# Attention and MLP on one core: the first batch on one queue in order of need, the later loads on the Pool queue

## The chip, the cores and the metric

The kernel runs on one core of one Trainium2 chip. The metric is the device time of one execution in microseconds (us). Each kernel was run several times; a run is called slow when it is over 1.5% above the fastest run of the same kernel, and the other runs fast. A verdict is "the same" when the interval of the ratio lies within 2%, and "unclear" when it lies on both sides of that line.

The engines go by the profile's names: PE is the TensorE (matmul), PEld its weight loads, DVE the VectorE, ACT the ScalarE, POOL the GpSimd engine, SP the SyncE. SP and ACT issue transfers to hardware queues, POOL to a software queue; the profile prints these kinds beside each queue. The clock granted to PE is printed as a share of full speed (PEclk). "L433" is line 433 of the kernel in question, so line numbers differ between kernels.

## The reference, cut to what matters

```python
# q, k, v: (8 batches, 8 heads, 576 positions, 64), float32
scores = q @ k^T / 8;  mask = |i - j| <= 32
attn = softmax(where(mask, scores, -1e9))
x = (attn @ v) as (4608 tokens, 512)
h = x @ w_in                       # 512 -> 2048
g = s * relu(h)**2 + b
out = g @ w_out                    # 2048 -> 512, float32
```

## The kernel before

For each batch the kernel loads q, k and v to staging tiles (`STG`), casts them to bf16 (`NAT`, `VB`), and needs q and k transposed (`QT`, `KT`). Batches 0 and 1 (`b < NPE`) are loaded in chunks of 256 rows and transposed on the TensorE. Batches 2 to 7 are loaded in blocks of 128 rows and transposed by DMA. Attention runs in units of 192 queries and two head pairs; the MLP runs in token blocks, the first of 384, 128 and 256 tokens. The attention of later batches is spread between the MLP's matmuls.

A planner puts all tasks into one fixed order for each engine, by assumed costs and a key. At run time each engine keeps to this order: in the traces of two kernels planned alike (below) PE, DVE and ACT ran the same 2544, 483 and 331 instructions in the same order, though their loads landed at different times. So the instruction at the head of an engine waits, and everything behind it too.

```python
def load(b, n, blk, waits=()):          # v of all batches; q and k of batches 2 to 7
    ...
    return add(
        "pool" if n == "v" else "sp",
        lambda e: e.dma_start(
            STG[n][p0:p1, blk, :].rearrange("p (h d) -> p h d", h=H),
            src_of[n][b, :, s0:s0 + ns, :].rearrange("h s d -> s h d"),   # pieces of 64 float32
        ), ...)

def load2(b, n, c, waits=()):           # q and k of batches 0 and 1, pieces of 128 float32
    s0, ns = CHUNKS[c]
    return add("sp", lambda e: e.dma_start(
        STG[n][0:ns, 2 * c:2 * c + 2, :].rearrange("p a (h x) -> p (a h) x", h=NPAIR),
        src_of[n][b, :, s0:s0 + 2 * ns, :].rearrange("h (p r) d -> p h (r d)", r=2)), ...)

for n, c in (("q", 0), ("k", 0), ("k", 1), ("q", 1), ("k", 2), ("q", 2)):
    load2(0, n, c)
for blk in range(6):
    load(0, "v", blk)
...
wts = [load_weights("in" if i < 4 else "out", i % 4) for i in range(8)]   # on "pool"
...
def transpose_dma(b, n, blk):
    ...
    add("sp", lambda e: e.dma_start(dst[:, :, c0:c0 + ns], NAT[n][0:ns, blk, :], transpose=True),
        1250.0, reads=[("NAT", n, blk)], writes=grans(n, slot, s0, s0 + ns), ...)
...
# batch 1 may not load before the sixth weight has landed
load2(b, *x, waits=[wts[5]] if b == 1 else ())
```

The softmax here doesn't subtract the row's maximum and nothing guards it: scores larger than these inputs give would overflow.

Of the kernel before, what the change touches and what calls it, by code (L numbers as in the profile page):

```python
# [6 lines left out]
BF16 = mybir.dt.bfloat16  # L7
# [204 lines left out]
def bass_sliding_window_symmetric__then__act_starrelu_kernel(  # L212
# [23 lines left out]
    with ExitStack() as es:  # L236
# [51 lines left out]
        EVACS = [("act", "dve"), ("dve", "dve")]  # L288
# [6 lines left out]
        for b in range(B - 1, 0, -1):  # L295
            for t in range(NT3 - 1, -1, -1):
                for g2 in (1, 0):
                    nxt = min(nxt - PACE, 16 * first_block(b * S + 192 * t) - LEAD)
                    rel[b, t, g2] = nxt

# [12 lines left out]
        def load(b, n, blk, waits=()):  # L313

            if n == "v":
                p0, p1 = VROWS[blk]
                s0 = 192 * (blk // 2) - WIN + 128 * (blk % 2) + p0
            else:
                p0, p1 = 0, rows(blk)
                s0 = 128 * blk  # L320
            ns = p1 - p0
            return add(
                "pool" if n == "v" else "sp",
                lambda e: e.dma_start(  # L324
                    STG[n][p0:p1, blk, :].rearrange("p (h d) -> p h d", h=H),
                    src_of[n][b, :, s0:s0 + ns, :].rearrange("h s d -> s h d"),
                ),
                900.0 if n == "v" else 1070.0, writes=[("STG", n, blk)], waits=waits,
                key=-2000 if b == 0 and n == "v" and blk < 2 else key_of(b, -5),
                dma=("v" if n == "v" else "l", ns * 9.4))  # L330
# [4 lines left out]
        def load2(b, n, c, waits=()):  # L335
            s0, ns = CHUNKS[c]
# [3 lines left out]
                    STG[n][0:ns, 2 * c:2 * c + 2, :].rearrange("p a (h x) -> p (a h) x", h=NPAIR),  # L340
                    src_of[n][b, :, s0:s0 + 2 * ns, :].rearrange("h (p r) d -> p h (r d)", r=2),
                ),
                1000.0, writes=[("STG", n, 2 * c), ("STG", n, 2 * c + 1)], key=key_of(b, -5), waits=waits,
                dma=("l", 8 * ns * 26 / 16.0))
# [14 lines left out]
        for n, c in (("q", 0), ("k", 0), ("k", 1), ("q", 1), ("k", 2), ("q", 2)):  # L359
            load2(0, n, c)  # L360
        for blk in range(6):
            load(0, "v", blk)
# [37 lines left out]
        wts = [load_weights("in" if i < 4 else "out", i % 4) for i in range(8)]  # L400


        def cast_v(b, blk):
# [5 lines left out]
                380.0, reads=[("STG", "v", blk)] + pad, writes=[("VB", slot, blk)], key=key)  # L409
            if blk in (2, 4):  # L410
                add("dve", lambda e: e.tensor_copy(VB[slot][0:64, blk, :], STG["v"][64:128, blk - 1, :]),
                    380.0, reads=[("STG", "v", blk - 1)], writes=[("VB", slot, blk)], key=key,
                    accum=False)

        def grans(n, slot, lo, hi):
            return [(n + "T", slot, x) for x in range(max(0, lo) // 64, (min(S, hi) - 1) // 64 + 1)]
# [6 lines left out]
        def transpose_dma(b, n, blk):  # L423
# [4 lines left out]
                1250.0, reads=[("NAT", n, blk)], writes=grans(n, slot, s0, s0 + ns),  # L428
                dma=("t", 1000.0), key=key_of(b, max(0, 128 * blk - WIN) // 192 - 0.4))

        def cast2(b, n, c):
            ns = CHUNKS[c][1]
            add("dve", lambda e: e.tensor_copy(  # L433
                NAT[n][0:ns, 2 * c:2 * c + 2, :].rearrange("p r (h d) -> p r h d", h=H),
                STG[n][0:ns, 2 * c:2 * c + 2, :].rearrange("p a (g r d) -> p r (a g) d", r=2, d=D)),
                700.0, reads=[("STG", n, 2 * c), ("STG", n, 2 * c + 1)],
                writes=[("NAT", n, 2 * c), ("NAT", n, 2 * c + 1)], key=key_of(b, c - 0.5))
# [3 lines left out]
        def transpose_pe(b, n, c, banks, evacs):  # L441
            slot = b % 2
            s0, ns = CHUNKS[c]
            dst = QT[slot] if n == "q" else KT[slot]
            c0 = s0 + (0 if n == "q" else WIN)
            key = key_of(b, c - 0.4)
            for r in range(2):
                res, bank = banks[tcount["n"] % len(banks)]
                tcount["n"] += 1
                view = bank.bitcast(BF16)[:, 0:512].rearrange("p (g c) -> p g c", g=NPAIR)[:, :, 0:ns]  # L450
                to = dst[:, :, c0:c0 + 2 * ns].rearrange("p g (x r) -> p r g x", r=2)[:, r]
                add("pe", [lambda e, pr=pr, r=r, view=view: e.transpose(  # L452
                    view[:, pr, :], NAT[n][0:ns, 2 * c + r, pr * 128:(pr + 1) * 128], IDENT[0:ns, 0:ns])
                    for pr in range(NPAIR)],
                    270, reads=[("NAT", n, 2 * c), ("NAT", n, 2 * c + 1), "IDENT"], writes=[res], key=key)
# [3 lines left out]
                add(evac, fn, 200 + 4 * ns / 1.0, reads=[res],  # L459
                    writes=grans(n, slot, s0, s0 + 2 * ns), key=key, accum=(r == 1))  # L460
# [5 lines left out]
        def unit(b, t, g2, after):  # L466
# [7 lines left out]
            qk_res = grans("q", slot, q0, q0 + 192) + grans("k", slot, q0 - WIN, q0 + 192 + WIN)  # L474
            qk_res.append(("KTPAD", slot))
            fns = []
            for u, pr in enumerate(prs):
# [14 lines left out]
                700.0, reads=[("E", e_), "MASK"], writes=[("E", e_)], key=key)  # L492
# [30 lines left out]
        for b in range(B):  # L523
# [3 lines left out]
            if b < NPE:  # L527
                steps = [("q", 0), ("k", 0), 0, ("k", 1), ("q", 1), 1, ("k", 2), ("q", 2), 2]
                if b > 0:
                    for x in steps:  # L530
                        if isinstance(x, tuple):
                            load2(b, *x, waits=[wts[5]] if b == 1 else ())
# [13 lines left out]
            for x in steps:  # L546
                if isinstance(x, tuple):
                    cast2(b, *x)
                    transpose_pe(b, *x, banks, EVACS[b])
                    continue  # L550
                cast_v(b, 2 * x)
                cast_v(b, 2 * x + 1)
# [137 lines left out]
```

## Time and profile before

| | before |
|---|---|
| time, median of 3 runs (range) | 345.61 us (345.03 to 349.01) |
| PE busy | 314.9 us of a span of 344.8 us |
| DMA transposes, issue to landing, median (largest) | qt 3.6 (7.5), kt 3.5 (8.7) us |
| first mask multiply, first MLP matmul | 20.77, 29.96 us |

From the page of the profile: the DMA queues (packets, megabytes, time of the packets as a share of 16 engines), and the chain of waits that ended last.

```profile
q1 hardware_dynamic: 100416, 35.40, 50.1%
q0 software_dynamic: 7360, 13.64, 20.3%
...
PE 83%; DMA 7%; DVE 4%; issue 2%; SPq 1%; ACT 1%; DVEq 0%
```

Two queues carry nearly everything: the hardware queue in small packets (35.40 MB over 100416 packets is 353 B each) and the software queue in large ones (1853 B each). The chain is 83% PE: the kernel is bound by the TensorE. Where PE is not full shows in windows of ten us. The columns are the window, then for PE, PEld, DVE, ACT and POOL the busy us and the number of instructions, then the granted clock of PE, the DMA share and GB/s.

```profile
10.00:20.00 10.00, 3.31 (x33) 2.50 (x31) 4.88 (x8) 3.21 (x4) 6.24 (x9) 1.00 1.15 221
20.00:30.00 10.00, 8.21 (x121) 5.71 (x119) 9.68 (x20) 8.08 (x15) 2.32 (x4) 1.00 1.24 208
...
60.00:70.00 10.00, 9.85 (x102) 5.81 (x101) 8.30 (x21) 4.43 (x12) 0.78 (x1) 1.00 0.92 221
90.00:100.00 10.00, 6.33 (x67) 3.37 (x65) 7.50 (x19) 5.94 (x12) 2.07 (x3) 1.00 1.25 195
110.00:120.00 10.00, 9.84 (x92) 4.72 (x92) 5.96 (x14) 5.16 (x9) 1.17 (x2) 1.00 1.20 186
120.00:130.00 10.00, 9.79 (x84) 4.71 (x84) 8.68 (x19) 7.93 (x14) 1.58 (x2) 1.00 1.27 223
130.00:140.00 10.00, 9.95 (x84) 4.53 (x84) 8.02 (x20) 7.35 (x14) 2.37 (x3) 1.00 0.84 173
```

PE is idle in the first 30 us and again at 90 to 100 us; elsewhere it is close to 10. The reason at the start is on DVE. In its timeline (start, duration, instruction, and in brackets the idle time before it and what ended it) the first v cast waits 5.10 us, and a cast of q waits 4.28 us, with the first mask multiply (L490) behind it at 20.77.

```profile
8.18 0.67 DVE L408 CAST vb<-stgv 128x512 bf16<-128x512 f32 x1 [5.10 <-DMA stgv<-in_v_dram]
...
18.97 0.69 DVE L433 CAST natq<-stgq 128x1024 bf16<-128x1024 f32 x1 [4.28 <-DMA stgq<-in_q_dram]
...
20.77 0.69 DVE L490 TENSOR_TENSOR ex<-ex,mask 128x1024 bf16<-128x1024 bf16 x1
```

The hole at 90 to 100 us begins with this wait of PE (us in total, times, longest), for one transpose that landed late:

```profile
PE sc L480 <- DMA kt<-natk: 3.4, 1, 3.4
```

The last view is of DMA between 85 and 250 us: transfers by tile, issuing engine, count, size, and the median from issue to landing. In this stretch all q and k loads and all transposes are on SP.

```profile
out_dram<-outs SPq DMA_DIRECT2D x18, 256.0 KB, 2.9
stgq<-in_q_dram SPq DMA_DIRECT2D x17, 256.0 KB, 5.4
stgk<-in_k_dram SPq DMA_DIRECT2D x17, 256.0 KB, 5.7
...
qt<-natq SPq DMA_TRANSPOSE x28, 3.6
kt<-natk SPq DMA_TRANSPOSE x28, 3.5
```

Loads take about 5.5 us, transposes about 3.5.

### The profile page before, as it was taken

Reading aid. Unit: us, or ns where it says so; the run is one execution under the profiler, and the core shown is the slowest. Engines: PE = TensorE matmul, PEld = TensorE weight load, DVE = VectorE, ACT = ScalarE, POOL = GpSimd, SP = SyncE. Lnnn points to the kernel's source line nnn. Section 1 sums busy time; section 2 is a strip of 40 time slices with the busy share of each in tenths; the row PEclk is TensorE's granted clock in tenths of the full one; section 3 lists DMA queues with packets and bytes.
Section 4 is the critical chain, followed back from the end, with each engine's and each line's share of the span. In section 5 each row is a group of like instructions: output and inputs, shape, how many; then the busy total and the mean of one; then the engine's idle time right before and its main releaser. Section 6 shows DMA issues by size and latency. Waiting matters only on the chain.

```text
span 344.8 us, 6390 instructions
## 1 busy us (share of the span) xinstructions
PE 314.9 (91%) x2504; PEld 159.8 (46%) x2544; DVE 211.2 (61%) x475; ACT 181.6 (53%) x327; POOL 48.1 (14%) x68
## 2 busy tenths in 40 slices
PE   0459999999869999999999999999999999999995
PEld 0345556565435444444444444444444444445542
DVE  2676578888958688768677677653445345433321
ACT  1357634476747586755667665653466355533310
POOL 8812041001305011202022000000000000000000
PEclk9999999999999999999999999999999999999999
DMA  7999999979998998997999997630000010010111
GB/s 192 235 211 206 212 250 195 223 168 183 237 165 182 202 219 180 200 206 147 206 204 185 209 205 168 140 75 32 31 32 30 32 61 32 22 41 30 62 50 75
DMA packets 107807, 49.46 MB, mean 143 GB/s; under 512 B 87552, under 2 KB 100864, under 8 KB 107776
## 3 DMA queue, kind: packets, MB, share of 16 engines
q1 hardware_dynamic: 100416, 35.40, 50.1%
q0 software_dynamic: 7360, 13.64, 20.3%
q8 instruction: 20, 0.33, 0.4%
q14 instruction: 11, 0.09, 0.1%
HBM read 36.70 MB, written 9.44 MB: 134 GB/s over the span
## 4 chain that ended last, share of the span: by engine, by line
PE 83%; DMA 7%; DVE 4%; issue 2%; SPq 1%; ACT 1%; DVEq 0%
PE w L572 36%; PE o L590 35%; DMA stgq<-in_q_dram 4%; PE ss L503 4%; PE sc L480 4%; PE av L503 3%; DMA kt<-natk 3%; PE o L611 1%; DVE vb L408 1%; DVE xt L517 1%; SPq L339 1%; ACT ex L487 1%; PE sc L452 1%; DVE ex L490 1%; DVE natk L420 0%
## 5 line engine op out<-in xcount | busy, mean ns | idle before, releaser
L572 PE MATMUL w<-xt,win 128*128 128x512 bf16 (+3 forms) x689 | 146.3, 342 | 2.3 <-issue 1.1
L590 PE MATMUL o<-wout,gt 128*128 128x512 bf16 x551 | 140.4, 379 | 2.1 <-issue 1.1
L572 PEld LDWEIGHTS w<-xt,win 128*128 128x128 bf16 x704 | 62.8, 98 | 61.1 <-DVE xt L517 0.9
L590 PEld LDWEIGHTS o<-wout,gt 128*128 128x128 bf16 x576 | 53.4, 98 | 58.2 <-DVE outs L602 0.5
L324 POOL DMA_DIRECT2D stgv<-in_v_dram x48 | 38.9, 812 | 140.5 <-DVE vb L408 121.0
L487 ACT ACTIVATE ex<-sc 128x1024 bf16<-128x1024 f32 x48 | 49.1, 1022 | 10.5 <-PE sc L480 9.6
L490 DVE TENSOR_TENSOR ex<-ex,mask 128x1024 bf16<-128x1024 bf16 x48 | 33.1, 691 | 21.6 <-ACT ex L487 21.2
L578 ACT ACTIVATE r_26<-w 128x512 bf16<-128x512 f32 (+3 forms) x44 | 22.9, 520 | 28.2 <-PE w L572 26.2
L578 ACT ACTIVATE r_25<-w 128x512 bf16<-128x512 f32 (+3 forms) x44 | 22.8, 518 | 26.2 <-PE w L572 24.0
L578 ACT ACTIVATE r_27<-w 128x512 bf16<-128x512 f32 (+3 forms) x44 | 22.8, 519 | 23.3 <-PE w L572 22.0
L578 ACT ACTIVATE r_28<-w 128x512 bf16<-128x512 f32 (+3 forms) x44 | 22.8, 519 | 23.1 <-PE w L572 23.0
L510 ACT ACTIVATE rec<-ss 128x384 f32<-128x384 f32 x48 | 23.4, 488 | 21.6 <-PE ss L503 21.5
L602 DVE SCALAR_TENSOR_TENSOR outs<-o,sb_33,cvec 128x512 f32<-128x512 f32 x36 | 26.9, 748 | 12.0 <-PE o L590 11.7
L517 DVE TENSOR_TENSOR xt<-av,rec 128x384 bf16<-128x384 f32 x48 | 26.6, 554 | 10.8 <-PE av L503 8.0
L581 DVE TENSOR_TENSOR gt<-r_26 128x512 bf16<-128x512 bf16 (+3 forms) x44 | 16.4, 374 | 21.5 <-ACT r_26 L578 21.3
L581 DVE TENSOR_TENSOR gt<-r_27 128x512 bf16<-128x512 bf16 (+3 forms) x44 | 16.4, 374 | 20.9 <-ACT r_27 L578 20.9
L581 DVE TENSOR_TENSOR gt<-r_28 128x512 bf16<-128x512 bf16 (+3 forms) x44 | 16.4, 373 | 18.4 <-ACT r_28 L578 18.1
L408 DVE CAST vb<-stgv 128x512 bf16<-128x512 f32 (+1 forms) x48 | 21.1, 445 | 8.4 <-DMA stgv<-in_v_dram 5.1
L513 ACT ACTIVATE rec<-rec 128x384 f32<-128x384 f32 x48 | 24.9, 519 | 0.7
L480 PE MATMUL sc<-qt,kt 64*128 64x128 bf16 x384 | 20.3, 229 | 3.7 <-DMA kt<-natk 3.4
L503 PE MATMUL ss<-ex,ones 128*64 128x128 bf16 x384 | 20.9, 234 | 1.5 <-DVE ex L490 1.5
L503 PEld LDWEIGHTS ss<-ex,ones 128*64 128x64 bf16 x384 | 12.8, 114 | 20.2 <-issue 5.3
(55 smaller groups left out, 153.6 us busy)
## 6 DMA issues: line engine op xcount, KB each, us to landing
out_dram<-outs SPq DMA_DIRECT2D x36, 256.0 KB, 2.3
stgq<-in_q_dram SPq DMA_DIRECT2D x24, 256.0 KB, 5.5
stgk<-in_k_dram SPq DMA_DIRECT2D x24, 256.0 KB, 5.5
stgv<-in_v_dram POOLq DMA_DIRECT2D x16, 256.0 KB, 6.8
stgv<-in_v_dram POOLq DMA_DIRECT2D x16, 192.0 KB, 6.6
stgq<-in_q_dram SPq DMA_DIRECT2D x4, 512.0 KB, 14.8
stgk<-in_k_dram SPq DMA_DIRECT2D x4, 512.0 KB, 12.8
stgv<-in_v_dram POOLq DMA_DIRECT2D x16, 128.0 KB, 6.3
```

The source lines that it names most:

```text
L324: lambda e: e.dma_start(STG[n][p0:p1, blk, :].rearrange("p (h d) -> p h d", h=H), src_of[n][b, :, s0:s0 + ns, :].rearrange("h s d -> s h d ...
L480: fns.append(lambda e, u=u, pr=pr, a=a, hh=hh: e.matmul(SC[:, hh, 256 * u + 128 * a:256 * u + 128 * a + 128], lhsT=KT[slot][64 * hh:64 * h ...
L487: add("act", lambda e: e.activation(EX[e_][:, :, :], SC[:, :, :], AF.Exp, bias=0.0, scale=0.125), 1040.0, reads=[("SC", 0), ("SC", 1)], wr ...
L490: add("dve", lambda e: e.tensor_tensor(EX[e_][:, :, :], EX[e_][:, :, :], MASK[:, :, :], ALU.mult), 700.0, reads=[("E", e_), "MASK"], write ...
L503: fns.append(lambda e, u=u, a=a, hh=hh, dst=dst, lhs=lhs: e.matmul(dst[64 * hh:64 * hh + 64, 192 * u + 64 * a:192 * u + 64 * a + 128], lhs ...
L513: add("act", lambda e: e.activation(REC[e_][:, :], REC[e_][:, :], AF.Exp, bias=0.0, scale=-1.0), 500.0, reads=[("REC", e_)], writes=[("REC ...
L517: add("dve", lambda e: e.tensor_tensor(XT[:, prs[0]:prs[1] + 1, x0:x0 + 192], AV[:, 0:384].rearrange("p (u c) -> p u c", u=2), REC[e_][:, ...
L572: add("pe", [lambda e, kc=kc: e.matmul(W[wb][:, 0:nt], lhsT=WIN_BF[:, kc, ft * 128:(ft + 1) * 128], rhs=XT[:, kc, t0:t0 + nt], start=(kc = ...
L578: add("act", lambda e: e.activation(R1[rb][:, 0:nt], W[wb][:, 0:nt], AF.Relu, bias=0.0, scale=1.0), 190 + 0.82 * nt, reads=[("W", wb)], wr ...
L581: add("dve", lambda e: e.tensor_tensor(GT[gs][:, ft, 0:nt], R1[rb][:, 0:nt], R1[rb][:, 0:nt], ALU.mult), 160 + 0.53 * nt, reads=[("R1", rb ...
L590: add("pe", [lambda e, fc=fc: e.matmul(O[ob][:, :], lhsT=GT[gs][:, fc, sub * 128:sub * 128 + 128], rhs=WOUT_BF[:, fc, :], start=(fc == 0), ...
L602: add("dve", lambda e: e.scalar_tensor_tensor(OUTS[us][:, :], O[ob][:, :], SB128[:, 0:1], CVEC[:, :], ALU.mult, ALU.add), 760, reads=[("O" ...
```

## The change

Intent: let attention of batch 0 start earlier, and free SP from the later loads so that it can issue transposes as soon as their casts are done.

1. First batch: q, k and v of batch 0 all go on SP, in order of need. Its first two 256-row chunks are divided by head halves, in load, cast and transpose. Casts of later chunks and of v are ordered behind the mask multiplies and score matmuls that matter more. The weights wait until the second q chunk has landed.
2. Later loads: the 60 loads of q and k of batches 2 to 7 go on Pool's queue, behind v. The transposes stay on SP.

```diff
-        def load(b, n, blk, waits=()):
+        def load(b, n, blk, waits=(), stream="pool"):
             return add(
-                "pool" if n == "v" else "sp",
+                stream,
...
+        HALVED = [(0, 0), (0, 1)]
+        WGATE = ("q", 1)
+        B1GATE = 5
...
-        for n, c in (("q", 0), ("k", 0), ("k", 1), ("q", 1), ("k", 2), ("q", 2)):
-            load2(0, n, c)
-        for blk in range(6):
-            load(0, "v", blk)
+        first = {}
+        for x in (("q", 0), ("v", 0), ("v", 1), ("q", 1), ("v", 2), ("v", 3), ("q", 2), ("v", 4), ("v", 5)):
+            if x[0] == "v":
+                first[x] = load(0, *x, stream="sp")
+                continue
+            for gr in parts2(0, x[1]):
+                for n in "qk":
+                    first[n, x[1]] = load2(0, n, x[1], gr)
...
-        wts = [load_weights("in" if i < 4 else "out", i % 4) for i in range(8)]
+        wts = [load_weights("in" if i < 4 else "out", i % 4, waits=[first[WGATE]])
+               for i in range(8)]
...                                   # in the loop over batches
-                    cast2(b, *x)
-                    transpose_pe(b, *x, banks, EVACS[b])
+                    aft = [("mask", 2 * x[1])] if b == 0 and x[1] > 0 else []
+                    for gr in parts2(b, x[1]):
+                        cast2(b, *x, gr, after=aft)
+                    for gr in parts2(b, x[1]):
+                        transpose_pe(b, *x, gr, banks, EVACS[b])
...
-                cast_v(b, 2 * x)
-                cast_v(b, 2 * x + 1)
+                cast_v(b, 2 * x, after=[("qk", 2 * x + 1)] if b == 0 else [])
+                cast_v(b, 2 * x + 1, after=[("qk", 2 * x + 1)] if b == 0 else [])
```

More of the change, by code (lines that the diff above doesn't have):

```diff
@@ L287, in bass_sliding_window_symmetric__then__act_starrelu_kernel @@
         NPE = 2
-        EVACS = [("act", "dve"), ("dve", "dve")]
+        HALVED = [(0, 0), (0, 1)]
+        WGATE = ("q", 1)
+        B1GATE = 5
+        CASTS = {"q": "dve", "k": "dve"}
+        EVACS = [("act", "dve"), ("dve", "dve"), ("dve", "dve")]
         def first_block(tok):
@@ L299, in bass_sliding_window_symmetric__then__act_starrelu_kernel @@
                     rel[b, t, g2] = nxt
+        STG2 = {n: STG[n][:, :, :].rearrange("p (c a) (h x) -> p c (a h) x", a=2, h=NPAIR) for n in "qk"}
         src_of = {"q": q, "k": k, "v": v}
@@ L327, in load, with parts2, load2 @@
                 ),
-                900.0 if n == "v" else 1070.0, writes=[("STG", n, blk)], waits=waits,
-                key=-2000 if b == 0 and n == "v" and blk < 2 else key_of(b, -5),
-                dma=("v" if n == "v" else "l", ns * 9.4))
+                900.0, writes=[("STG", n, blk)], waits=waits, key=key_of(b, -5),
+                dma=("v" if stream == "pool" else "l", ns * 9.4))
         CHUNKS = [(256 * c, min(128, (S - 256 * c) // 2)) for c in range((S + 255) // 256)]
-        def load2(b, n, c, waits=()):
-            s0, ns = CHUNKS[c]
+        def parts2(b, c):
+            return [(0, 2), (2, 4)] if (b, c) in HALVED else [(0, 4)]
+        def load2(b, n, c, g, waits=()):
+            (s0, ns), (g0, g1) = CHUNKS[c], g
             return add(
@@ L339, in load2 @@
                 lambda e: e.dma_start(
-                    STG[n][0:ns, 2 * c:2 * c + 2, :].rearrange("p a (h x) -> p (a h) x", h=NPAIR),
-                    src_of[n][b, :, s0:s0 + 2 * ns, :].rearrange("h (p r) d -> p h (r d)", r=2),
-                ),
-                1000.0, writes=[("STG", n, 2 * c), ("STG", n, 2 * c + 1)], key=key_of(b, -5), waits=waits,
-                dma=("l", 8 * ns * 26 / 16.0))
+                    STG2[n][0:ns, c, 2 * g0:2 * g1, :],
+                    src_of[n][b, 2 * g0:2 * g1, s0:s0 + 2 * ns, :].rearrange(
+                        "h (p r) d -> p h (r d)", r=2),
+                ),
+                300.0 + 180.0 * (g1 - g0),
+                writes=[("STG", n, 2 * c + x) for x in range(g0 // 2, (g1 + 1) // 2)],
+                key=key_of(b, -5), waits=waits, dma=("l", 2 * (g1 - g0) * ns * 24 / 16.0))
         def load_weights(which, i, waits=()):
@@ L398, in bass_sliding_window_symmetric__then__act_starrelu_kernel, with cast_v @@
             reads=["MASK"], writes=["MASK"], key=key_of(0, -0.3))
-        wts = [load_weights("in" if i < 4 else "out", i % 4) for i in range(8)]
-        def cast_v(b, blk):
+        wts = [load_weights("in" if i < 4 else "out", i % 4, waits=[first[WGATE]])
+               for i in range(8)]
+        def cast_v(b, blk, after):
             slot = b % 2
@@ L408, in cast_v @@
             add("dve", lambda e: e.tensor_copy(VB[slot][p0:128, blk, :], STG["v"][p0:128, blk, :]),
-                380.0, reads=[("STG", "v", blk)] + pad, writes=[("VB", slot, blk)], key=key)
+                380.0, reads=[("STG", "v", blk)] + pad, writes=[("VB", slot, blk)], key=key, after=after)
             if blk in (2, 4):
@@ L412, in cast_v @@
                     380.0, reads=[("STG", "v", blk - 1)], writes=[("VB", slot, blk)], key=key,
-                    accum=False)
+                    after=after)
         def grans(n, slot, lo, hi):
@@ L427, in transpose_dma, with cast2, transpose_pe @@
             add("sp", lambda e: e.dma_start(dst[:, :, c0:c0 + ns], NAT[n][0:ns, blk, :], transpose=True),
-                1250.0, reads=[("NAT", n, blk)], writes=grans(n, slot, s0, s0 + ns),
-                dma=("t", 1000.0), key=key_of(b, max(0, 128 * blk - WIN) // 192 - 0.4))
-        def cast2(b, n, c):
-            ns = CHUNKS[c][1]
-            add("dve", lambda e: e.tensor_copy(
-                NAT[n][0:ns, 2 * c:2 * c + 2, :].rearrange("p r (h d) -> p r h d", h=H),
-                STG[n][0:ns, 2 * c:2 * c + 2, :].rearrange("p a (g r d) -> p r (a g) d", r=2, d=D)),
-                700.0, reads=[("STG", n, 2 * c), ("STG", n, 2 * c + 1)],
-                writes=[("NAT", n, 2 * c), ("NAT", n, 2 * c + 1)], key=key_of(b, c - 0.5))
+                1250.0, reads=[("NAT", n, blk)], writes=[x + (y,) for x in grans(n, slot, s0, s0 + ns) for y in range(2)],
+                dma=("t", 1200.0), key=key_of(b, max(0, 128 * blk - WIN) // 192 - 0.4))
+        def cast2(b, n, c, g, after=()):
+            ns, (g0, g1) = CHUNKS[c][1], g
+            sl = range(g0 // 2, (g1 + 1) // 2)
+            to = NAT[n][0:ns, 2 * c:2 * c + 2, 128 * g0:128 * g1].rearrange("p r (h d) -> p r h d", d=D)
+            of = STG2[n][0:ns, c, 2 * g0:2 * g1, :].rearrange("p h (r d) -> p r h d", r=2)
+            eng = CASTS[n] if b == 0 else "dve"
+            add(eng, (lambda e: e.copy(to, of)) if eng == "act" else (lambda e: e.tensor_copy(to, of)),
+                100 + (150.0 if eng == "dve" else 230.0) * (g1 - g0), reads=[("STG", n, 2 * c + x) for x in sl],
+                writes=[("NAT", n, 2 * c + x) for x in sl], key=key_of(b, c - 0.5), after=after)
         tcount = {"n": 0}
-        def transpose_pe(b, n, c, banks, evacs):
+        def transpose_pe(b, n, c, g, banks, evacs):
             slot = b % 2
-            s0, ns = CHUNKS[c]
+            (s0, ns), (g0, g1) = CHUNKS[c], g
             dst = QT[slot] if n == "q" else KT[slot]
@@ L446, in transpose_pe @@
             key = key_of(b, c - 0.4)
+            sl = range(g0 // 2, (g1 + 1) // 2)
             for r in range(2):
@@ L449, in transpose_pe @@
                 tcount["n"] += 1
-                view = bank.bitcast(BF16)[:, 0:512].rearrange("p (g c) -> p g c", g=NPAIR)[:, :, 0:ns]
-                to = dst[:, :, c0:c0 + 2 * ns].rearrange("p g (x r) -> p r g x", r=2)[:, r]
+                view = bank.bitcast(BF16)[:, 0:512].rearrange("p (g c) -> p g c", g=NPAIR)[:, g0:g1, 0:ns]
+                to = dst[:, g0:g1, c0:c0 + 2 * ns].rearrange("p g (x r) -> p r g x", r=2)[:, r]
                 add("pe", [lambda e, pr=pr, r=r, view=view: e.transpose(
-                    view[:, pr, :], NAT[n][0:ns, 2 * c + r, pr * 128:(pr + 1) * 128], IDENT[0:ns, 0:ns])
-                    for pr in range(NPAIR)],
-                    270, reads=[("NAT", n, 2 * c), ("NAT", n, 2 * c + 1), "IDENT"], writes=[res], key=key)
+                    view[:, pr - g0, :], NAT[n][0:ns, 2 * c + r, pr * 128:(pr + 1) * 128],
+                    IDENT[0:ns, 0:ns]) for pr in range(g0, g1)],
+                    70 * (g1 - g0), reads=[("NAT", n, 2 * c + x) for x in sl] + ["IDENT"],
+                    writes=[res], key=key)
                 evac = evacs[r]
@@ L458, in transpose_pe @@
                       (lambda e, to=to, view=view: e.tensor_copy(to, view)))
-                add(evac, fn, 200 + 4 * ns / 1.0, reads=[res],
-                    writes=grans(n, slot, s0, s0 + 2 * ns), key=key, accum=(r == 1))
+                add(evac, fn, 220 + (g1 - g0) * ns / 1.0, reads=[res],
+                    writes=[x + (y,) for x in grans(n, slot, s0, s0 + 2 * ns) for y in sl], key=key,
+                    accum=(r == 1))
         ucount = {"n": 0}
@@ L473, in unit @@
             q0 = 192 * t
-            qk_res = grans("q", slot, q0, q0 + 192) + grans("k", slot, q0 - WIN, q0 + 192 + WIN)
+            qk_res = [x + (g2,) for x in grans("q", slot, q0, q0 + 192)
+                      + grans("k", slot, q0 - WIN, q0 + 192 + WIN)]
             qk_res.append(("KTPAD", slot))
@@ L491, in unit @@
                                                  ALU.mult),
-                700.0, reads=[("E", e_), "MASK"], writes=[("E", e_)], key=key)
+                700.0, reads=[("E", e_), "MASK"], writes=[("E", e_)], key=key, name=("mask", n))
             for (dst, res) in ((SS, "SS"), (AV, "AV")):
@@ L527, in bass_sliding_window_symmetric__then__act_starrelu_kernel @@
             if b < NPE:
-                steps = [("q", 0), ("k", 0), 0, ("k", 1), ("q", 1), 1, ("k", 2), ("q", 2), 2]
+                steps = [("q", 0), ("k", 0), 0, ("q", 1), ("k", 1), 1, ("q", 2), ("k", 2), 2]
                 if b > 0:
@@ L531, in bass_sliding_window_symmetric__then__act_starrelu_kernel @@
                         if isinstance(x, tuple):
-                            load2(b, *x, waits=[wts[5]] if b == 1 else ())
+                            load2(b, *x, (0, 4), waits=[wts[B1GATE]] if b == 1 else ())
                     for blk in range(6):
```

## The prediction

> **What bounds the kernel now.** From about 36 us on it is the TensorE. The chain of waits is 83% PE, and the windows of ten us show 9.4 to 9.95 us of PE work in each from 30 to 340 us, except 90-100 (6.33). Two places leave PE idle.
>
> 1. The start: 0.49, 3.31 and 8.21 us busy in the first three windows. The timeline shows an order problem on VectorE. It sits until 8.2 us on the first v cast (idle 5.1 us), although q chunk 0 landed at about 5.3. After the first exp (done 16.4) it waits with the cast of q chunk 1 until 19.0 (idle 4.3 us), so the first mask multiply runs only at 20.8. The first MLP matmul comes at 29.96. PE is cold until then: four 128x384 matmuls take 1.46 us at 30 us, 0.82 us at 34 us (the Trainium skill, "TensorE: Matmul & The Clock Gate", Part 1, has this half rate; the clock row of this profile does not show it).
> 2. At 96.7 us PE waits 3.4 us for kt: that DMA transpose was issued at 91.4, behind loads on SP, and took 8.67 us (median 3.5).
>
> **What DMA does.** In the queue table cut into 2 us, the hardware queue alone moves 0.54-0.59 MB per 2 us. Beside weights it gets 0.13-0.14 (16-20 us), beside v loads 0.06 (38-42 us). The skill ("DMA: Bandwidth & Descriptors", Queues, rings and completion order) says engines alternate between queues by packet; the software queue's packets here average 1853 B, hardware loads 512 or 256 B, which agrees.
>
> **What the change does.** (a) Gated weights leave q0, k0, v0, v1, q1 (about 2 MB) alone on the hardware queue: estimated at its own rate, q1 lands at about 11 us instead of 19. (b) Head halves let casts, transposes and evacuations (0.68, 1.03, 0.73 us per whole piece) overlap; the explicit orders keep masks ahead of later casts. Cost: two more loads, casts and some small evacuations, about 1-2 us of DVE/ACT, partly hidden. (c) Weights start about 4-5 us later but meet less competition; the bytes are the same, so they end at about 36 us as before, the batch-1 gate (33.4) perhaps 2 us earlier. (d) 60 q/k loads move from SP to Pool, at 0.8 us issue each, about 48 us on an engine that is 14% busy; SP then issues transposes right after their casts. Against that, transposes meet more large software packets (8.1 us each at 106-112, beside v loads).
>
> **Critical share.** First MLP matmul: estimate 21 us instead of 30. Attention of batch 0 ends about 27 instead of 36.5. That is 9 us. MLP work without batch 1 (about 31 us) would then run out at about 55; batch 1 now lands at 47-57 because of the weights, and its first xt (68.6) can hardly come before 58-61. So 1-4 us go back. The 96 us stall should shrink by 1-3 us. After 110 us PE is full; nothing changes.
>
> 345.6 - 9 + 2.5 (batch 1 late) + 1 (more small work) - 2 (kt stall) - 2 (warmer PE) = **336 us**; 80% range 328 to 343. Faster by over 2%: 0.70; within 2%: 0.25; slower: 0.05.
>
> **What would show it.** First mask multiply near 10 us, no DVE wait of 4-5 us before 20; first MLP matmul 19-23; last weight landing 35-38; 20-30 us window of PE at 9 or more; kt waits under 2 us; transposes median up, to 4-6 us; windows after 110 us unchanged.
>
> **What would make it wrong.** PE stalls at 45-65 us for batch 1 that give most back; transposes of batch 2 starved by software loads, with stalls of 5 us or more at 75-95; Pool loads blocked in order behind v buffers; weights late, so that MLP starts early but waits.

## More of the kernel before

`NAT` and `STG` have one copy, so the cast of the next batch waits until the transpose has read `NAT`, and the next load waits for that cast.

## The result, and the profile after

The kernel after took 379.54 us (median of 6 runs, 372.58 to 385.68; three of the six called slow), the kernel before 345.66 us in the same rounds (6 runs, 343.85 to 349.01). The ratio is 1.083, 95% interval 1.073 to 1.093: slower by 8%. Here and below a ratio is the mean time of one kernel's fast runs over that of the other's fast runs of the same rounds, so it is not quite the ratio of the quoted medians. The profile shown is of a fast run, with a span of 370.8 us.

| | before | after |
|---|---|---|
| first mask multiply | 20.77 us | 11.44 us |
| first MLP matmul | 29.96 us | 25.18 us |
| qt transposes, issue to landing, median (largest) | 3.6 (7.5) us | 12.2 (26.1) us |
| kt transposes, the same | 3.5 (8.7) us | 11.8 (31.2) us |

The change of the first batch shows on DVE, in the same timeline as before. The first multiply by the mask (L514) is 9 us earlier, and no wait of 4 to 5 us is left before 20 us:

```profile
11.44 0.69 DVE L514 TENSOR_TENSOR ex<-ex,mask 128x1024 bf16<-128x1024 bf16 x1
...
20.08 0.71 DVE L425 CAST vb<-stgv 128x512 bf16<-128x512 f32 x1
```

But the chain of waits is now only 49% PE, and a third of it is DMA. The bytes on the software queue went from 13.64 to 26.62 MB:

```profile
q0 software_dynamic: 11392, 26.62, 41.6%
q1 hardware_dynamic: 48928, 22.42, 36.2%
...
PE 49%; DMA 32%; SPq 7%; DVE 4%; issue 4%; POOL 3%; POOLq 0%; DVEq 0%
```

The windows tell where. PE is busier from 10 to 20 us (6.81 for 3.31), and 90 to 100 us is fuller (9.11 for 6.33). Then come 60 to 70 us (5.29 for 9.85) and 110 to 150 us, where four windows add to 27.03 us for 39.42, so 12.4 us of PE busy time are missing. The lost work is more than that: in two of the windows shown the granted clock was 0.83 and 0.85, which makes a busy PE slower. At 110 to 120 us the core moved 82 GB/s, less than half of before, with the DMA engines as occupied as before (1.13 for 1.20).

```profile
10.00:20.00 10.00, 6.81 (x82) 4.26 (x76) 8.35 (x18) 6.69 (x13) 6.60 (x9) 1.00 1.17 222
20.00:30.00 10.00, 7.83 (x81) 4.51 (x82) 7.42 (x16) 5.94 (x12) 5.38 (x7) 1.00 1.23 202
...
60.00:70.00 10.00, 5.29 (x54) 2.78 (x52) 3.94 (x11) 3.04 (x7) 2.99 (x4) 0.94 0.89 212
90.00:100.00 10.00, 9.11 (x107) 5.02 (x105) 9.83 (x22) 6.37 (x11) 8.70 (x11) 1.00 1.08 171
110.00:120.00 10.00, 7.58 (x53) 3.54 (x51) 2.54 (x8) 3.98 (x9) 1.77 (x2) 1.00 1.13 82
120.00:130.00 10.00, 6.27 (x48) 2.64 (x48) 6.78 (x15) 1.45 (x2) 5.97 (x8) 0.83 1.10 235
130.00:140.00 10.00, 7.13 (x69) 3.43 (x66) 3.31 (x6) 5.08 (x9) 2.08 (x3) 0.85 1.22 106
```

The DMA view of the same stretch, 85 to 250 us, as before. The transposes did not change queue, yet they take 13 us for 3.5; the output stores on SP take 12.9 for 2.9; the loads that were moved take 12 for 5.5.

```profile
stgq<-in_q_dram POOLq DMA_DIRECT2D x17, 256.0 KB, 12.3
stgk<-in_k_dram POOLq DMA_DIRECT2D x17, 256.0 KB, 11.7
out_dram<-outs SPq DMA_DIRECT2D x14, 256.0 KB, 12.9
...
qt<-natq SPq DMA_TRANSPOSE x26, 13.4
kt<-natk SPq DMA_TRANSPOSE x26, 13.2
```

One of the transposes, in the timeline of SP. Its issue alone occupied SP for 14.34 us, and it landed 31.2 us after its start:

```profile
110.04 14.34 SPq L445 DMA_TRANSPOSE kt<-natk  x1
```

From there the delay runs on to PE. DVE waits with the cast that would overwrite `NAT`, since the transpose has not yet read it; PE waits for DVE, which has the mask multiply (`ex`), the squared relu (`gt`) and the attention result (`xt`) behind that cast. These are the waits of DVE for transposes (before: none), and those of PE:

```profile
DVE natk L438 <- DMA kt<-natk: 16.1, 5, 5.2
DVE natq L438 <- DMA qt<-natq: 12.3, 7, 3.7
```

```profile
PE ss L527 <- DVE ex L514: 15.2, 7, 4.7
PE o L617 <- DVE gt L608: 6.2, 2, 5.5
PE w L599 <- DVE xt L541: 4.5, 3, 2.8
```

The same in the chain that ended last (start, us, what). Three of the four pieces shown are transposes of 16 to 25 us. The first, at 43.44, is the second k chunk of batch 1, on SP in 512-B pieces, while batch 2 loads on Pool: its cast runs at 66.75 us (before: 59.13; with the same order and the loads on SP, an experiment below: 61.86), which is the hole at 60 to 70 us.

```profile
43.44 23.29 DMA stgk<-in_k_dram
...
97.57 25.34 DMA qt<-natq
...
128.65 19.07 DMA kt<-natk
...
166.79 16.43 DMA kt<-natk
```

### The profile page after: what moved, and what is told of

It reads as the page before. It is cut to its first block, busy times and chain, and to the rows that moved or that the text cites. A ratio compares the mean times of both kernels' runs of the same rounds, so it can differ in the third digit from the quotient of the medians.

```text
span 370.8 us, 6532 instructions
## 1 busy us (share of the span) xinstructions
PE 327.7 (88%) x2544; PEld 161.6 (44%) x2544; DVE 214.7 (58%) x483; ACT 182.7 (49%) x331; POOL 95.4 (26%) x122
## 3 DMA queue, kind: packets, MB, share of 16 engines
q0 software_dynamic: 11392, 26.62, 41.6%
## 4 chain that ended last, share of the span: by engine, by line
PE 49%; DMA 32%; SPq 7%; DVE 4%; issue 4%; POOL 3%; POOLq 0%; DVEq 0%
PE o L617 23%; PE w L599 21%; DMA kt<-natk 10%; DMA stgk<-in_k_dram 8%; DMA stgv<-in_v_dram 7%; DMA qt<-natq 7%; SPq L445 4%; SPq L349 3%; PE ss L527 2%; PE sc L504 2%; PE av L527 2%; POOL stgq L331 1%; POOL stgk L331 1%; SPq L331 1%; DVE vb L425 1%
## 5 line engine op out<-in xcount | busy, mean ns | idle before, releaser
L617 PE MATMUL o<-wout,gt 128*128 128x512 bf16 x576 | 147.3, 387 | 8.9 <-DVE gt L608 6.2
L599 PE MATMUL w<-xt,win 128*128 128x512 bf16 (+3 forms) x704 | 151.0, 348 | 4.5 <-DVE xt L541 4.5
L605 ACT ACTIVATE r<-w 128x512 bf16<-128x512 f32 (+3 forms) x176 | 89.8, 519 | 110.1 <-PE w L599 106.1
L608 DVE TENSOR_TENSOR gt<-r 128x512 bf16<-128x512 bf16 (+3 forms) x176 | 63.8, 373 | 67.0 <-ACT r L605 65.4
L514 DVE TENSOR_TENSOR ex<-ex,mask 128x1024 bf16<-128x1024 bf16 x48 | 32.9, 688 | 18.6 <-ACT ex L511 18.3
L331 POOL DMA_DIRECT2D stgk<-in_k_dram x30 | 25.6, 854 | 43.6 <-DVE natk L438 17.6
L331 POOL DMA_DIRECT2D stgq<-in_q_dram x30 | 25.8, 862 | 42.2 <-DVE natq L438 29.1
L541 DVE TENSOR_TENSOR xt<-av,rec 128x384 bf16<-128x384 f32 x48 | 26.5, 553 | 10.9 <-PE av L527 7.2
L629 DVE SCALAR_TENSOR_TENSOR outs<-o,sb,cvec 128x512 f32<-128x512 f32 x36 | 26.9, 746 | 9.7 <-PE o L617 9.4
L527 PEld LDWEIGHTS ss<-ex,ones 128*64 128x64 bf16 x384 | 12.9, 114 | 34.7 <-DVE ex L514 19.7
L438 DVE CAST natk<-stgk 128x512 bf16<-128x512 f32 (+1 forms) x30 | 14.4, 480 | 16.1 <-DMA kt<-natk 16.1
L527 PE MATMUL av<-ex,vb 128*64 128x128 bf16 x384 | 20.4, 232 | 0.2
L438 DVE CAST natq<-stgq 128x512 bf16<-128x512 f32 (+1 forms) x30 | 12.6, 421 | 12.4 <-DMA qt<-natq 12.3
## 6 DMA issues: line engine op xcount, KB each, us to landing
stgq<-in_q_dram POOLq DMA_DIRECT2D x24, 256.0 KB, 10.9
stgk<-in_k_dram POOLq DMA_DIRECT2D x24, 256.0 KB, 11.2
stgv<-in_v_dram POOLq DMA_DIRECT2D x14, 256.0 KB, 11.2
```

What stands on the lines that cost most here:

```text
L331: lambda e: e.dma_start(STG[n][p0:p1, blk, :].rearrange("p (h d) -> p h d", h=H), src_of[n][b, :, s0:s0 + ns, :].rearrange("h s d -> s h d ...
L438: add("dve", lambda e: e.tensor_copy(NAT[n][0:ns, blk, :], STG[n][0:ns, blk, :]), 400.0, reads=[("STG", n, blk)], writes=[("NAT", n, blk)] ...
L514: add("dve", lambda e: e.tensor_tensor(EX[e_][:, :, :], EX[e_][:, :, :], MASK[:, :, :], ALU.mult), 700.0, reads=[("E", e_), "MASK"], write ...
L527: fns.append(lambda e, u=u, a=a, hh=hh, dst=dst, lhs=lhs: e.matmul(dst[64 * hh:64 * hh + 64, 192 * u + 64 * a:192 * u + 64 * a + 128], lhs ...
L599: add("pe", [lambda e, kc=kc: e.matmul(W[wb][:, 0:nt], lhsT=WIN_BF[:, kc, ft * 128:(ft + 1) * 128], rhs=XT[:, kc, t0:t0 + nt], start=(kc = ...
L605: add("act", lambda e: e.activation(R1[rb][:, 0:nt], W[wb][:, 0:nt], AF.Relu, bias=0.0, scale=1.0), 190 + 0.82 * nt, reads=[("W", wb)], wr ...
```

## The experiments

Fifteen kernels ran, each on one chip beside runs of the kernel before. Compare ratios, not medians.

Theory 1: the software queue's large packets starve the DMA transposes, whose packets are small. The Trainium skill ("DMA: Bandwidth & Descriptors", Queues, rings and completion order) says that a DMA engine serves its queues in turn, a packet at a time; the same page (SWDGE vs HWDGE vs iDMA) puts a packet at 4096 B or less by preference. The packet records of the kernel after agree with the sizes: between 85 and 250 us most software packets are of 4096 B and the transposes' packets of 256 B. If turns alternate, a transpose gets one packet per 4096-B packet of the loads. The records do not name a packet's engine, so no run here shows the turns themselves. An estimate from the records: a transpose of 128 KB is 512 packets of 256 B, 32 on each of 16 engines, and 32 turns of 396 and 41 ns, the mean times of the two kinds of packet, are 14 us.
Rivals, numbered as in the expectations: (2) the new first batch, its late weights and the planner's new order cost the time; (3) Pool's queue delivers the loads too late, however fast the transposes are; (4) any second queue beside the transposes costs them their share, whatever its packets.

### Each part alone

First part only, the 60 loads back on SP:

```diff
-        def load(b, n, blk, waits=(), stream="pool"):
+        def load(b, n, blk, waits=(), stream=None):
+            stream = stream or ("pool" if n == "v" else "sp")
...                                   # and the planner's cost of these loads as before
```

> Only the first-batch part of the change; q and k loads of batches 2 to 7 back on SP. Theory 1 (the software loads' 4096-byte packets starve the 256-byte packets of the DMA transposes): 333 to 345 us, transposes landing in 3 to 5 us, no PE stall over 4 us after 80 us. Rival 2 (the new first batch, its late weights and the new static order cost the time): over 360 us. Rival 3 (the Pool queue delivers the loads too late) expects the same as theory 1 here.

Measured: 347.32 us (344.81 to 350.51), before 345.34; ratio 1.004 (0.995 to 1.013), the same, and slower than the 333 to 345 us of theory 1. Transposes 4.2 us.

Second part only, from the kernel before:

```diff
-                "pool" if n == "v" else "sp",
+                "pool",
...
-                dma=("v" if n == "v" else "l", ns * 9.4))
+                dma=("v", ns * 9.4))
```

> The kernel before with nothing changed but the q and k loads of batches 2 to 7 on the Pool queue. Theory 1 and rival 3: 365 to 385 us, transposes of the median over 10 us, PE stalls of 5 us and more at 100 to 190 us. Rival 2: 343 to 350 us.

Measured: 382.69 us (369.52 to 394.12). Three of its four runs are called slow, so it has no ratio; its only fast run, 369.52 us, is above every run of before (343.26 to 347.96). Its profile is of a slow run: transposes 11.2 and 11.3 us, PE waiting 19.0 us for `ex`. The second part alone brings the loss; rival 2 falls as far as it blames the first batch. What the first part was meant to gain is not there either, which is taken up below.

### The same order, another queue

Here the plan is made as in the kernel after, and the 60 loads are given to another engine only then. The instructions on PE, DVE and ACT stand in exactly the order of the kernel after; a comparison of the instruction lists shows no line changed.

```diff
         g.plan()
+        for t in moved:                       # the 60 loads of q and k
+            t.stream, t.dma = "sp", ("l", t.dma[1])
```

> The changed kernel with the order of instructions on PE, VectorE and ScalarE kept exactly, the 60 q and k loads moved from Pool to SP at the place in the order that they had. Theory 1: 334 to 348 us, transposes 3 to 5 us. Rival 2, as far as it blames the static order of the engines: 370 us or more.

Measured: 346.12 us (345.26 to 347.81), ratio 1.003 (0.996 to 1.011), against 1.083 for the kernel after. It was run at another time. In the DMA view from 85 to 250 us everything is fast again, although loads and transposes now share one queue:

```profile
stgq<-in_q_dram SPq DMA_DIRECT2D x17, 256.0 KB, 4.8
stgk<-in_k_dram SPq DMA_DIRECT2D x17, 256.0 KB, 4.4
...
kt<-natk SPq DMA_TRANSPOSE x28, 4.6
qt<-natq SPq DMA_TRANSPOSE x27, 4.9
```

This is the cleanest pair: with the order unchanged, the queue of 60 loads makes the 8%. Rival 2 falls for the order as well.

### Loads and transposes kept apart in time

The kernel after, with every load of batch b waiting until all DMA transposes of batch b-1 have landed. Batch 1 has none, so the loads of batch 2 are not held.

```diff
+                held = tr.get(b - 1, [])
-                        load(b, n, blk)
+                        load(b, n, blk, waits=held)
```

> The changed kernel, loads still on Pool, but the loads of batch b wait until all transposes of batch b-1 have landed, so that the two kinds are never in flight together (from batch 3 on). Theory 1: transposes land in 2.5 to 4 us at the median, 340 to 358 us. Rival 3: loads come still later, so 375 us or more, though the transposes are quick.

Measured: 353.79 us (353.59 to 356.80), ratio 1.027 (1.019 to 1.035, unclear at 2%), transposes 6.8 and 5.0 us; the loads of q and k land in 5.7 and 6.0 us (after: 10.9 and 11.2). Less overlap, less loss, on the very same queue. The transposes are slower than the 2.5 to 4 us expected: the two were not fully apart, since loads of v still meet transposes of their own batch. Rival 3, which expected 375 us or more, falls; nor did any cast of batches 2 to 7 (L438) wait for its load in the kernel after.

The loss that is left arises where nothing was held apart, before batch 3. DVE waits 8.05 us for the second k chunk of batch 1, which is loaded beside batch 2, and PE waits 6.37 us behind it:

```profile
67.04 0.69 DVE L455 CAST natk<-stgk 128x1024 bf16<-128x1024 f32 x1 [8.05 <-DMA stgk<-in_k_dram]
```

By a count of the matmul work from the trace, like the one further below, this run is 7.5 us behind the same-order kernel at 80 us and 5.6 at 200; the spans differ by 7.2. From 80 us on, where loads and transposes were kept apart, nothing more is lost.

### A separate hardware queue, small packets

As the same-order kernel, with the 60 loads on ScalarE's queue.

```diff
-            t.stream, t.dma = "sp", ("l", t.dma[1])
+            t.stream, t.dma = "act", ("l", t.dma[1])
```

> The changed kernel with the order on PE and VectorE kept exactly; the 60 q and k loads are issued from ScalarE's hardware queue in place of Pool, so still a queue apart from that of the transposes, but with 256-byte packets. Theory 1 (it is the size of the software packets that starves the transposes): transposes 3 to 6 us at the median and DMA at 180 GB/s or more from 100 to 200 us; the time 343 to 360 us, as ScalarE pays for 60 issues and their waits. Rival 4 (any second queue beside the transposes halves their share): transposes 8 us or more, 360 us or more.

Measured: 360.22 us (359.79 to 360.48), ratio 1.042 (1.035 to 1.050), transposes 5.3 and 5.2 us. A queue of their own does not starve the transposes when the packets are of 256 B. The kernel still loses 4%. ScalarE now has 60 issues with their waits in its stream, and the trace shows them reaching PE:

```profile
PE w L604 <- ACT r L610: 7.6, 4, 4.0
```

The same-order kernel has no such wait. The longest, 4.0 us, ends at 61.81, just after one load's issue had held ScalarE for 6.93 us, from 54.50. This is read from the trace; no run tests it. Rival 4 falls for the transposes and stays possible for a part of the time.

### Packet size, by itself

So far packet size and kind of queue had changed together. Two kernels change the size on ScalarE's hardware queue alone: the loads read contiguous pieces of 2048 B or 512 B, so the wrong elements; bytes, order and destination stay. (Both pass the comparison with the reference all the same, so that comparison would not notice wrong elements of q and k; q and k are drawn with a spread of 0.1, so the scores are small and the softmax is almost even.) A third does the same to the kernel after, on Pool: its packets stay at 4096 B, but hold two pieces of 2048 B in place of sixteen of 256 B.

```diff
-                    src_of[n][b, :, s0:s0 + ns, :].rearrange("h s d -> s h d"),
+                    src_of[n][b].rearrange("h s d -> (h s d)").rearrange(
+                        "(a r x) -> r a x", a=1, r=S)[s0:s0 + ns],     # a=1: 2048 B, a=4: 512 B
```

> Wrong result on purpose. As the run with the 60 loads on ScalarE's hardware queue (transposes 5.3 and 5.2 us median, 360.2 us, packets of 256 B), same order of instructions, same bytes, but each load reads 2048 contiguous bytes per row, so the same queue carries packets of about 2048 B. Packet size starves the transposes: their median goes to 8 to 12 us, DMA time in the chain rises, and the kernel is 365 to 380 us although the loads themselves have an eighth of the packets. The rival, that the software queue as such is what starves them: transposes stay at 4 to 5.5 us and the time at or below 360.

Measured: transposes 14.3 and 11.8 us; 362.79 us (362.32 to 364.87), before 345.64, ratio 1.050 (1.045 to 1.054). The queue line, and the DMA view from 85 to 250 us:

```profile
q10 hardware_dynamic: 7872, 14.16, 22.1%
```

```profile
stgq<-in_q_dram ACTq DMA_DIRECT2D x17, 256.0 KB, 14.1
...
out_dram<-outs SPq DMA_DIRECT2D x14, 256.0 KB, 11.9
...
qt<-natq SPq DMA_TRANSPOSE x27, 15.4
kt<-natk SPq DMA_TRANSPOSE x27, 13.8
```

A seventh of the packets (7872 for 56256) for the same 14.16 MB, and transposes, stores and loads all take as long as with the software queue. Size is what starves them; the kind of queue is not. How it does so is less clear: the estimate by turns gives 7.6 us here (32 turns of 199 and 38 ns), and 20 us if the v loads on the software queue (390 ns) take a turn as well. The time fell short of the 365 to 380 us that was expected.

> Wrong result on purpose. As the previous run, with 512 contiguous bytes per piece. Packet size: transposes at 5.5 to 7 us, between the runs with 256 B (5.3) and 2048 B. Rival, the software queue as such: no change against 256 B, 4.5 to 5.5 us, and time at or below 360.

Measured (the DMA view from 85 to 250 us first):

```profile
kt<-natk SPq DMA_TRANSPOSE x27, 4.5
qt<-natq SPq DMA_TRANSPOSE x26, 4.9
```

Over the whole run transposes 4.9 and 4.5 us; 355.93 us (353.03 to 359.74), ratio 1.029 (1.020 to 1.038). The landing that packet size was expected to give, 5.5 to 7 us, did not come: 512 B are no worse than 256 B. The effect begins somewhere between 512 and 2048 B.

> Wrong result on purpose. The kernel after, loads on the Pool queue, reading 2048 contiguous bytes per row as in the first run of this call. The software queue's packets stay at about 4096 B, so packet size expects transposes at 11 to 13 us and about 380 us, as after. If it is rather the small pieces inside a software packet (sixteen of 256 B) that make it slow, packets of two pieces take much less than the 500 to 800 ns and the transposes come down to 4 to 8 us, with the time below 365.

Measured: transposes 15.4 and 14.8 us, in a slow run (the only one profiled); 365.76 us (359.77 to 372.63, two of four runs slow), ratio 1.043 (1.036 to 1.049). Larger pieces inside a packet do not help the transposes, nor do they shorten the packets: 406 ns on average between 85 and 250 us, against 396. (The 500 to 800 ns of the expectation are means of single stretches of 4 us, such as 621 at 108 to 112 us of the kernel after.) The time is lower than that of the kernel after, with landings no shorter, and that was expected by neither side.

| 60 loads on | packets, B | qt, kt landing, median us | ratio to before |
|---|---|---|---|
| SP, the transposes' own queue | 256 | 4.9, 4.6 | 1.003 |
| ScalarE, hardware queue | 256 | 5.3, 5.2 | 1.042 |
| ScalarE, hardware queue | 512 | 4.9, 4.5 | 1.029 |
| ScalarE, hardware queue | 2048 | 14.3, 11.8 | 1.050 |
| Pool, software queue, pieces of 2048 B | 4096 | 15.4, 14.8 (slow run) | 1.043 |
| Pool, software queue (after) | 4096 | 12.2, 11.8 | 1.083 |

The table also says what is not settled. Landing and time do not go in step: the last three rows have much the same landings and lose 4 to 8%, and rows two and three lose 3 to 4% with short ones. Of the loss of the kernel after, the comparison on one chip that comes nearest to the landing alone (2048 B against 512 B, 362.79 against 355.93) is worth about 7 us; it is not pure, since 60 issues also took ScalarE 24.5 us against 39.9. Why the rest differs stays open. The kernels with starved transposes on Pool also spread widely from run to run (13 us after, 13 us in the last kernel, 25 us with the second part alone, against 5 us before).

The traces do say where PE's time went. From 30 us on, PE was idle 26.6 us in the kernel after and 8.9 in the same-order kernel. And the clock granted to it fell to half for five stretches of 3.4 us, at 52, 69, 123, 137 and 188 us, each within 1.5 us of the end of a PE wait of 2.2 to 5.5 us; the same-order kernel has no such stretch. At half speed these 17.1 us cost up to 8.5 us, an estimate; with the 17.7 us of idle time that makes 26.2, and the spans differ by 25.8. With packets of 2048 B it is 8.5 us of idle time and again 8.5, for a difference of 15.9. So up to a third of the loss is PE running slowly after its waits, and equal landings cost these two kernels different amounts of waiting.

### Where the earlier start went

The first part alone brings the first MLP matmul to 24.47 us (before 29.96), yet the time is the same. I counted the matmul work that PE had issued by a given time, at its nominal duration, from the weight loads in the trace:

| us | 30 | 40 | 50 | 60 | 100 | 120 |
|---|---|---|---|---|---|---|
| before | 4.2 | 11.8 | 21.6 | 30.4 | 61.3 | 80.4 |
| first part only | 7.6 | 15.8 | 23.3 | 30.4 | 64.6 | 81.8 |

A lead of 4.0 us at 40 us is gone at 60. (At 100 us there is a lead of 3.3 again, as this run lacks the hole at 90 us; at 110 to 120 us PE is busy 8.49 us for 9.84, and the lead shrinks to 1.4.) In the trace of that run, PE waits 2.16 us at 50.14 for `CVEC`, which DVE computes late because it had waited for v of batch 1; then the granted clock is half for 3.4 us (51.03 to 54.44; eight matmuls of 128 columns take 1.06 us then, 0.61 after), about 1.7 us of work. The two add to 3.9 us, as much as the lead; that they are what ended it is argued. Theory 5: batch 1 comes too late for a PE that is ahead, because its loads wait for the sixth weight; let it land earlier and the gain stays. Rival 6: the planner assumes that loads land sooner than they do, so casts stand at the head of DVE and wait.

Three kernels test theory 5, all with the first part only. The first also moves v of batch 1 to SP, in order of need; the second does so and lets batch 1 load after the third weight; the third does only the latter.

```diff
-        B1GATE = 5
+        B1GATE = 2          # second and third kernel
...
+                        if isinstance(x, tuple) and x[0] == "k":      # first and second kernel
+                            for blk in (2 * x[1], 2 * x[1] + 1):
+                                load(b, "v", blk, waits=gate, stream="sp")
```

> The first-batch part alone (as in e1_first_only) plus one more step: the v loads of batch 1 also stand on SP, in order of need behind q and k of their chunk, so that no software loads run beside them after the weights. Theory 5 (the 9 us gained at the start are given back because chunk 0 of batch 1 lands at about 50 us, behind weights and software v loads): chunk 0 is cast by 43 to 46 us, the first 256-wide MLP matmul comes at 58 to 63 us instead of about 68, the time is 335 to 342 us. Rival 6 (the static order on PE and VectorE eats them): no gain, 344 to 349 us.

> As e6_b1_on_sp, with the loads of batch 1 released by the third weight load in place of the sixth. Theory 5: chunk 0 lands some 5 us earlier again (estimate 37 to 41 us, as hardware loads get about 70 GB/s beside weights), weights end 3 to 5 us later; 332 to 342 us. Rival 6: 344 us or more.

> The first-batch part alone with only the gate of batch 1 moved from the sixth weight load to the third; v of batch 1 stays on Pool. Theory 5: chunk 0 of batch 1 cast at 41 to 46 us, 336 to 343 us. Rival 6: 344 us or more.

Measured: 347.11 us (344.85 to 350.30), 347.79 us (346.14 to 349.57) and 346.10 us (345.50 to 346.52), before 347.55; ratios 1.002 (0.992 to 1.013), 1.006 (0.996 to 1.017) and 1.002 (0.994 to 1.009). In the first, the first cast of batch 1 runs at 42.8 us for 50.3, so batch 1 is 7.5 us earlier, and nothing is gained: DVE next waits 3.61 us with the cast of batch 2's q at its head, and by 100 us PE has done 63.8 us of work. Theory 5 falls as an explanation of the whole.

The next four change what comes behind. Theory 7: DMA is full until about 120 us, so batch 2 cannot come sooner however early PE starts. Two kernels transpose batch 2 on PE also (`NPE = 3`), with the first part and from the kernel before, to take its DMA transposes away. One keeps the first part and lets the planner assume loads 2 us slower (`DMALAT` 600 to 2600). One joins `NPE = 3` with v of batch 1 on SP.

```diff
-        NPE = 2
+        NPE = 3             # first, second and fourth kernel
...
-    DMALAT = 600.0
+    DMALAT = 2600.0         # third kernel
```

> The first-batch part alone, with batch 2 also transposed on PE (and loaded in 512-byte pieces) in place of ten DMA transposes. Theory 7 (the gain of the start is eaten because DMA is full until about 120 us, and batch 2 cannot be there sooner however early PE starts): less DMA work before 120 us shows as more PE work done by 120 us (at least 3 us more than the 81.8 of e1_first_only) and 338 to 344 us. Rival 6 (static order on VectorE, casts that wait at the head of the queue): no change, 345 to 349 us.

> The kernel before with batch 2 transposed on PE: the control of the run above. If the first-batch part is worth something once batch 2 comes sooner, this one is slower than e9_first_npe3 by 2 to 6 us; if it is worth nothing, they agree within 2 us. Theory 7 expects 341 to 346 us.

> The first-batch part alone, with the planner's own figure for the time from a DMA's end to its use raised from 0.6 to 2.6 us, so that the static order places casts later and they wait less at the head of VectorE's queue. Rival 6: VectorE's waits for DMA shrink and the time falls to 338 to 343 us. Theory 7: 344 to 349 us.

> All of batch 1 on SP (as e6_b1_on_sp) and batch 2 transposed on PE. Theory 7: the two reliefs add, 334 to 342 us. Rival 6: 345 us or more.

Measured, before 345.70 us: 352.86 us (351.78 to 355.85), ratio 1.025 (1.020 to 1.031); 349.08 us (348.54 to 351.30), 1.015 (1.010 to 1.020); 346.75 us (345.73 to 351.48), 1.007 (1.001 to 1.012); 351.15 us (349.25 to 352.04), 1.018 (1.013 to 1.024). Within 2% the second and third are the same as before, the other two unclear. More transposes on PE gain nothing with or without the first part, and with it the time is 3.8 us longer than without, where theory 7 expected it to be shorter: it falls. The slower assumption gains nothing either, so rival 6 in this form falls too. No kernel beat the one before; why a lead of 4 us cannot be kept until 120 us stays open.

## Why the prediction was wrong, point by point

**What bounds the kernel: right.** PE, the two holes and their causes were read correctly. The hole at 90 us was indeed filled (9.11 for 6.33), but others opened.

**"That is 9 us" at the start: mis-sized, and worthless.** The first mask multiply came at 11.44 us, near the 10 that was predicted. The first MLP matmul came at 25.18 us, not 21. In the trace the last v casts stand at 18.06 to 20.71 us ahead of the masks of the second chunk, at up to 0.72 us each (0.43 at 10.12), and Pool was issuing weights and loads then; no run tests whether that is the cause. The lead of PE measured 4 us at 40 us in the run with the first part only, and 0 at 60. The prediction took back 2.5 us for a late batch 1 where all was given back.

**"- 2 (kt stall)": the step that failed.** The prediction let the later loads' move to Pool (d) gain 2 us, by prompt issue, "Against that, transposes meet more large software packets", at "transposes median up, to 4-6 us". They went up to 12, the largest to 31: where the prediction took 2 us off, the move cost 26 us of span against the same-order kernel (370.8 against 345.0). With the order on PE, DVE and ACT unchanged, the queue of those loads alone is worth 8% (1.083 against 1.003). The competition stood in the prediction; its size had been measured and was not used. The prediction itself quotes a transpose of 8.1 us beside v loads. And beside the weights, the hardware queue got 0.13 to 0.14 MB per 2 us in place of 0.54 to 0.59, a quarter. An estimate from these numbers, 3.5 us times four, is 14 us for a transpose, and 12 was measured; that it is so near is partly luck, since beside v loads the queue got still less (0.06). The quarter was applied to the start alone.

**"After 110 us PE is full; nothing changes": wrong.** 110 to 150 us lost 12.4 us of PE busy time. PE had been full there while transposes landed in 3.5 us; that it would stay full with slower ones was assumed, not read.

**"Transposes of batch 2 starved by software loads, with stalls of 5 us or more at 75-95"** was named among what would make it wrong. It did not come there: at 70 to 90 us PE was full (9.96 and 10.00 us). The stalls came at 60 to 70 us, where PE waited 4.7 us behind batch 1's k, a load beside batch 2's loads on Pool, and from 97 us with the transposes. The prediction gave slower by over 2% a chance of 5%.

**Shown, argued, open.** Shown: the queue of the loads makes the loss; large packets, not the software queue as such, make transposes about three times as slow; the first part is neutral. Argued from the trace: the way from late transposes through casts at the head of DVE to PE and its clock, the cost of ScalarE's issues, and how the early lead is lost by 60 us. Open: by what turns large packets delay small ones, why equal landings make PE wait 8.5 us more in one kernel and 17.7 in another, and what keeps an earlier start from paying.

## What to carry to other kernels

Before moving transfers to another queue, look at what stays behind: here DMA transposes of 256-B packets took about three times as long beside packets of 2 to 4 KB on another queue, and a tight plan had no room for that latency. If two streams must share the engines, put the large one on the same queue as the latency-bound one or keep them apart in time, and judge by the landing times of the transfers that did not move and by the waits of the engine that bounds the kernel. When a trace shows how one queue fares beside another, use that factor on everything that will stand in the same place, not only on the stage where it was read; and an early lead counts only if every later stage can take it.

## What the Trainium skill lacked or had wrong

- "DMA: Bandwidth & Descriptors", Issuing engines are not separate DMA queues, and Rules for kernel authors: both say that issuing from several engines saves only issue time. Here the choice of queue is not neutral: the same instructions in the same order took 8% longer (ratio 1.083 against 1.003) with 60 loads on Pool rather than SP, and 4% with them on ScalarE.
- The same page, Rules for kernel authors: "A transpose next to ordinary DMAs needs nothing". For correctness the runs say little: all passed, but so did those that read wrong elements of q and k. For time it lacks that transposes of 256-B packets went from 3.5 to 12 us (up to 31) beside loads of 4096-B packets, and to 12 to 15 us beside 2048-B packets on a hardware queue, but stayed at 4.5 to 5.3 us beside 256 or 512 B.
- The same page, Queues, rings and completion order, states the turns by packet, which no run here contradicts or shows, but not what mixing costs in total: at 110 to 120 us the kernel after moved 82 GB/s (before 186), and a 4096-B packet took 396 ns on average between 85 and 250 us, against 306 before.
